# Guard and next threshold in one VectorE operation, and two arrays for the exact heads' transposed tiles, in an attention and mixture-of-experts kernel

## The chip, the cores and the metric

The kernel runs on one core of one Trainium2 chip, in one launch. The metric is device microseconds of one execution; a time is the median of several runs on the same chip. The engines are TensorE (PE in the profile, its weight loads PEld), VectorE (DVE), ScalarE (ACT), GpSimd (POOL) and SyncE (SP, which issues most DMAs). Each engine works through its own instructions in the order in which the program gives them; semaphores make one wait for another.

## The reference

Attention over 2 batches, 8 heads, 576 positions and head dimension 64, then two mixtures of experts. The change lies in the attention alone.

```python
scores = scale * np.matmul(q, k.transpose(0, 1, 3, 2))
thresh = np.max(scores, axis=-1, keepdims=True) - tau
scores = np.where(scores >= thresh, scores, -1000000000.0)
scores = scores - np.max(scores, axis=-1, keepdims=True)
attn = np.exp(scores)
attn = attn / (np.sum(attn, axis=-1, keepdims=True) + 1e-09)
return np.matmul(attn, v).astype(np.float32)
```

The output, 1152 rows of 512, goes through a mixture with 8 experts whose weights come from a softmax with 8 rounds of row and column normalization, and through one with 4 experts whose weights are given. Each expert is relu(x @ w1) @ w2 with 1024 hidden columns. All of it is float32.

## The kernel before, in words

Attention is cut into 72 units of 128 query rows. For each unit the scores against all 576 keys are one tile of two PSUM halves of 288 columns. `units` 0 to 15 are the first 256 query rows of the 8 heads of batch 0 and are called exact: their probabilities and values stay in float32. Units 0 to 3 of these (the first pair of heads, `ws`) have scores that are scaled only afterwards. Units 16 to 35 are the other 320 rows of batch 0, units 36 to 71 the rows of batch 1. These 56 units are not exact: each operand is split into a rounded high part and a remainder (float32r), and products are put together from several matmuls.

`step` (L421) is a software pipeline over the units. In step t unit t is `d` (mask, guard, norm), unit t+1 is `a` (maximum, threshold, exponential), unit t+2 is `nxt` (scores), and units t-2 to t-5 are `x`, `c`, `z`, `y` (transposes and products with the values). The calls in `step` are the order of the work on each engine:

- TensorE: `turn` of `x` (five transposes of the 576 probabilities, four into the PSUM bank et, the last 64 keys into the bank er; there is one bank of each), an exact head's products in three parts (`mix`, L367), filler matmuls, the scores (L282), a non-exact head's products (L374, L376), more filler.
- VectorE: `mask` (L309: scores at or above the threshold keep their exponential, and the sum comes out as an accumulator, which is read by an instruction of its own), `top` (L287, the maximum), `guard` (L313, the sum plus 1e-9), for exact units the threshold (L295, for `ws` units L297 and L298), `norm`'s reciprocal (L317), and then `lo` (L349 and L352, the remainders of the transposed tile), `low` and `rest` of finished heads (L387, L401) and the filler's remainder (L536, tile hl).
- ScalarE: `hi` (L334 copies the transposed tile to SBUF, and after a head's last unit L336 copies the remaining 64 keys), `out` (L384, L398), the exponential (L303 or L305), for the 56 units that are not exact the threshold (L292), the filler's relu (L533, tile hh), and then copies that split operands.
- GpSimd: `norm`'s multiplication (L319), and the remainders of split operands.

`st` holds a unit's maximum, threshold, sum, guarded sum and reciprocal, a column each, in six buffers. All exact heads put their transposed tiles into one array, `e32`: the first head of a pair in its columns 0 to 255, the second in 256 to 511. The heads that are not exact use `eth`, with the remainders in an array that takes `e32`'s place later (for the first such pair, in `tails`).

The filler (`expert_fill`, L527 and L555) is matmul work of the first two experts, which starts at step 20; `pull` gives each step a fixed number of portions, by `few`, `RA1` and `RA2`. What the steps have not done of it is done behind the attention. `cook` splits expert weights on ScalarE (L107) and GpSimd (L109), and `side` issues the loads of weights and calls it.

Of the kernel before, what the change touches and what calls it, by code (L numbers as in the profile page):

```python
# [19 lines left out]
P = 128  # L20
# [9 lines left out]
def attention_two_moe_kernel(ctx, tc, qP, kP, qT, kT, vp, tau, wg, w1, w1s, w2, w2s, dp, m2w1s, m2w2, m2w2s, out):  # L30
# [91 lines left out]
    class Attention:  # L122
# [5 lines left out]
        def __init__(self, pl, ps_s, ps_t, ps_r, ps_m):  # L128
# [7 lines left out]
            self.eth = pl.tile([P, 5, 640], F32R, name="eth")  # L136
            self.e32 = pl.tile([P, 5, 512], F32, tag="etl", name="e32")
            self.etl = None
            self.qz = [pl.tile([P, 3 * D], F32R, name=f"qz{i}") for i in range(2)]
# [145 lines left out]
        def top(self, u):  # L285
            st = u["st"] = self.pl.tile([P, 8], F32, tag="st", name="st", bufs=6)
            V.tensor_reduce(st[:, 0:1], u["sc"][:, :, :HS], axis=AX.XY, op=ALU.max, negate=not u["q"][0][0]["ws"])  # L287

        def line(self, u):
            st = u["st"]  # L290
            if not u["q"][0][0]["exact"]:
                A.activation(st[:, 2:3], st[:, 0:1], AF.Identity, bias=on[:, 1:2], scale=-1.0)  # L292
                return
            if not u["q"][0][0]["ws"]:
                V.tensor_scalar(st[:, 2:3], st[:, 0:1], -1.0, on[:, 0:1], op0=ALU.mult, op1=ALU.subtract)  # L295
                return
            V.tensor_scalar(st[:, 1:2], st[:, 0:1], lin[:, 0:1], None, op0=ALU.mult)  # L297
            V.tensor_scalar(st[:, 2:3], st[:, 0:1], lin[:, 1:2], None, op0=ALU.subtract)  # L298

        def exp(self, u):  # L300
            ex = u["ex"] = self.pl.tile([P, 2, HS], F32, tag="ex", name="ex", bufs=4)
            if u["q"][0][0]["ws"]:
                A.activation(ex, u["sc"][:, :, :HS], AF.Exp, bias=u["st"][:, 1:2], scale=esc)  # L303
            else:
                A.activation(ex, u["sc"][:, :, :HS], AF.Exp, bias=u["st"][:, 0:1])  # L305

        def mask(self, u):
            st, ex = u["st"], u["ex"]
            V.scalar_tensor_tensor(ex, u["sc"][:, :, :HS], st[:, 2:3], ex, op0=ALU.is_ge, op1=ALU.mult,  # L309
                                   accum_out=st[:, 3:4])  # L310

        def guard(self, u):
            V.tensor_scalar(u["st"][:, 4:5], u["st"][:, 3:4], 1e-9, None, op0=ALU.add)  # L313

        def norm(self, u):
            st = u["st"]
            V.reciprocal(st[:, 5:6], st[:, 4:5])  # L317
            exf = u["exf"] = u["ex"].rearrange("p a b -> p (a b)")
            G.tensor_scalar(exf, exf, st[:, 5:6], 1.0, op0=ALU.mult, op1=ALU.mult)  # L319
# [10 lines left out]

        def hi(self, u):
# [1253 lines left out]
```

## Time and profile before

| | |
|---|---|
| median of 3 runs | 1287.21 us (1286.96 to 1287.28) |
| the profiled execution | 1287.24 us, span 1285.5 us |
| TensorE busy | 1268.6 us (99%), 9373 matmuls |
| VectorE busy | 878.0 us (68%), 1843 instructions |
| ScalarE busy | 738.0 us (57%), 1491 instructions |
| GpSimd busy | 897.4 us (70%), 987 instructions |
| granted TensorE clock | 1.00 in all slices |

The attention stage is the first 240 us or so of the span; the mixtures fill the rest. Times in the trace count from the start of the span. A matmul's end in the trace is modelled, so a busy TensorE is not TensorE at its peak. An instruction of VectorE may start while the one before it still shows as busy. A line such as L80 or L85 is a helper's, and the tile names tell what it works on.

### The profile page before, as it was taken

Reading aid. Unit: us, or ns where it says so; the run is one execution under the profiler, and the core shown is the slowest. Engines: PE = TensorE matmul, PEld = TensorE weight load, DVE = VectorE, ACT = ScalarE, POOL = GpSimd, SP = SyncE. Lnnn points to the kernel's source line nnn. Section 1 sums busy time; section 2 is a strip of 40 time slices with the busy share of each in tenths; the row PEclk is TensorE's granted clock in tenths of the full one; section 3 lists DMA queues with packets and bytes.
Section 4 is the critical chain, followed back from the end, with each engine's and each line's share of the span. In section 5 each row is a group of like instructions: output and inputs, shape, how many; then the busy total and the mean of one; then the engine's idle time right before and its main releaser. Section 6 shows DMA issues by size and latency. Waiting matters only on the chain.

```text
span 1285.5 us, 25112 instructions
## 1 busy us (share of the span) xinstructions
PE 1268.6 (99%) x9373; PEld 1209.0 (94%) x9373; DVE 878.0 (68%) x1843; ACT 738.0 (57%) x1491; POOL 897.4 (70%) x987
## 2 busy tenths in 40 slices
PE   8998999999999999999999999999999999999998
PEld 5597988889889999999999999999989999999998
DVE  6798888566637666666666666666745666666667
ACT  7887887423546555554655555466546465556552
POOL 7997987415796767867676786767668578677760
PEclk9999999999999999999999999999999999999999
DMA  5542330101221112211111221111212012111102
GB/s 170 162 126 77 97 98 17 42 1 34 81 67 50 42 42 58 58 34 51 50 42 42 58 59 34 50 50 42 58 38 62 17 53 57 35 55 50 42 18 74
DMA packets 43226, 73.84 MB, mean 57 GB/s; under 512 B 5217, under 2 KB 12513, under 8 KB 43105
## 3 DMA queue, kind: packets, MB, share of 16 engines
q1 hardware_dynamic: 42816, 71.96, 19.6%
q8 instruction: 74, 1.21, 0.4%
q14 instruction: 48, 0.39, 0.1%
q10 hardware_dynamic: 288, 0.28, 0.1%
HBM read 69.86 MB, written 2.36 MB: 56 GB/s over the span
## 4 chain that ended last, share of the span: by engine, by line
PE 89%; DVE 6%; ACT 2%; POOL 1%; issue 1%; DMA 1%; SPq 0%; DVEq 0%; POOLq 0%; ACTq 0%
PE mm L1123 36%; PE mm L1435 33%; PE mm L555 5%; PE mm L527 4%; PE mm L1243 3%; PE mm L282 2%; PE mm L327 2%; DVE ex L309 1%; PE mm L367 1%; DVE st L287 1%; PE mm L376 1%; DVE etl L349 1%; PE mm L374 1%; ACT ex L305 0%; DVE hl L536 0%
## 5 line engine op out<-in xcount | busy, mean ns | idle before, releaser
L85 POOL TENSOR_TENSOR wl<-raw,wh 128x512 fp32r<-128x512 f32 x217 | 282.9, 1310 | 180.2 <-ACT wh L80 166.9
L1223 DVE SCALAR_TENSOR_TENSOR acc<-mm,p,acc 128x256 f32<-128x256 f32 (+1 forms) x428 | 195.3, 508 | 72.5 <-PE mm L1435 59.6
L1435 PE MATMUL mm<-wh,h 128*128 128x256 f32 x960 | 173.6, 280 | 0.0
L1130 ACT COPY snap<-mm 128x576 f32<-128x576 f32 x126 | 80.8, 642 | 157.4 <-DVE mm L1284 77.8
L80 ACT CAST wh<-raw 128x512 fp32r<-128x512 f32 x217 | 133.4, 627 | 47.1 <-PE mm L1435 26.4
L1435 PEld LDWEIGHTS mm<-wh,h 128*128 128x128 f32 x960 | 146.7, 188 | 0.0
L1123 PE MATMUL mm<-xh,wl 128*128 128x288 f32 x672 | 146.3, 299 | 0.3
L1123 PE MATMUL mm<-xh,wh 128*128 128x288 f32 x672 | 143.6, 295 | 0.0
L1123 PE MATMUL mm<-xl,wh 128*128 128x288 f32 x672 | 143.1, 294 | 0.0
L1435 PE MATMUL mm<-wl,h 128*128 128x256 f32 x480 | 134.8, 281 | 0.0
L1435 PE MATMUL mm<-wh,tails 128*128 128x256 f32 x696 | 126.4, 280 | 0.0
L85 POOL TENSOR_TENSOR wl<-sum,wh 128x512 fp32r<-128x512 f32 x82 | 107.0, 1305 | 8.1 <-ACT wh L80 8.1
L1123 PEld LDWEIGHTS mm<-xh,wl 128*128 128x128 f32 x672 | 106.4, 188 | 2.8 <-DVE mm L1143 0.5
L1123 PE MATMUL mm<-xth,wl 128*128 128x288 f32 x504 | 108.3, 296 | 0.1
L1123 PEld LDWEIGHTS mm<-xl,wh 128*128 128x128 f32 x672 | 107.9, 188 | 0.0
L1123 PEld LDWEIGHTS mm<-xh,wh 128*128 128x128 f32 x672 | 107.8, 188 | 0.0
L1123 PE MATMUL mm<-xtl,wh 128*128 128x288 f32 x504 | 107.8, 295 | 0.0
L1123 PE MATMUL mm<-xth,wh 128*128 128x288 f32 x504 | 107.7, 295 | 0.0
L1435 PEld LDWEIGHTS mm<-wh,tails 128*128 128x128 f32 x696 | 106.3, 188 | 0.0
L80 ACT CAST wh<-sum 128x512 fp32r<-128x512 f32 x82 | 51.5, 628 | 85.4 <-POOL sum L820 71.9
L1435 PE MATMUL mm<-wl,tails 128*128 128x256 f32 x348 | 97.4, 280 | 0.0
L1435 PEld LDWEIGHTS mm<-wl,h 128*128 128x128 f32 x480 | 90.3, 188 | 0.4
(242 smaller groups left out, 3489.5 us busy)
## 6 DMA issues: line engine op xcount, KB each, us to landing
raw<-in_w1s SPq DMA_DIRECT2D x56, 256.0 KB, 2.7
raw<-in_w2s SPq DMA_DIRECT2D x48, 256.0 KB, 2.6
raw<-in_w SPq DMA_DIRECT2D x40, 256.0 KB, 3.1
raw<-in_m2w1s SPq DMA_DIRECT2D x32, 256.0 KB, 2.7
raw<-in_m2w2s SPq DMA_DIRECT2D x28, 256.0 KB, 2.6
kr<-in_kT SPq DMA_DIRECT2D x22, 288.0 KB, 3.0
vr<-in_vp SPq DMA_DIRECT2D x24, 160.0 KB, 2.3
qr<-in_qT SPq DMA_DIRECT2D x8, 288.0 KB, 2.9
```

The lines of the kernel that those rows point to most:

```text
L80: A.copy(hi, src)
L85: el.tensor_tensor(lo, src, f(hi), op=ALU.subtract)
L282: T.matmul(sc[:m, hf, :HS], lhsT=q, rhs=kk[:, hf * HS:(hf + 1) * HS], start=i == 0, stop=i == len(ops) - 1)
L287: V.tensor_reduce(st[:, 0:1], u["sc"][:, :, :HS], axis=AX.XY, op=ALU.max, negate=not u["q"][0][0]["ws"])
L327: T.transpose(et[:, kt], exf[:, kt * P:(kt + 1) * P], ident)
L527: T.matmul(ph[:, :n], lhsT=a[:, kt * P:(kt + 1) * P], rhs=x[:, kt, n0:n0 + n], start=i == 0 and kt == 0, stop=i == 2 and kt == KT - 1)
L555: T.matmul(py, lhsT=x, rhs=a, start=i == 0, stop=i == 3 * FT - 1)
L1123: T.matmul(ch[b][:, g, :HS], lhsT=w[:, (2 * g + kt) * P:(2 * g + kt + 1) * P], rhs=operand(u, kt, lo), start=first and j == 0, stop=j == l ...
L1130: A.copy(v[u], m)
L1223: V.scalar_tensor_tensor(a, src, s, a, op0=ALU.mult, op1=ALU.add)
L1243: T.matmul(py, lhsT=hid[x][:, kk, o:o + P], rhs=w[y], start=n == 0, stop=n == 3 * HF - 1)
L1435: T.matmul(m, lhsT=hid(x, kt + ko), rhs=wk[y], start=first and n == 0, stop=n == 5, skip_group_check=True)
```

## The change

The threshold and the guard of all units that are exact but not `ws`, and of all units that are not exact, become one `tensor_tensor` on two columns: it takes the pair (sum of unit t, a constant) minus the pair (-1e-9, negated maximum of unit t+1) and so gives the guarded sum of unit t and the threshold of unit t+1. For this the sums and maxima lie in one tile, `sums`, of six places with eight columns each, in place of `st`; column 2 is set to -1e-9 by a memset and column 1 to the constant at the end of step 0. The threshold of the units that are not exact thereby goes from ScalarE to VectorE. `ws` units keep their separate operations. The tile that `eth` had becomes `e2`, a second array for exact heads: pairs 0 and 2 use `e2`, pairs 1 and 3 `e32`. `eth` is made when the first unit that is not exact is copied, in the place of `e2`. For exact heads the copy of the remaining keys goes from ScalarE (in `hi`) to VectorE (in `lo`).

```diff
--- before.py
+++ after.py
@@ -133,9 +133,11 @@
             self.later, self.late = [], []
             self.iq = self.iv = self.lq = self.lv = 0
             self.xf = {}
-            self.eth = pl.tile([P, 5, 640], F32R, name="eth")
+            self.e2, self.eth = pl.tile([P, 5, 640], F32, tag="eth", name="e2"), None
             self.e32 = pl.tile([P, 5, 512], F32, tag="etl", name="e32")
             self.etl = None
+            self.sums = pl.tile([P, 6, 8], F32, name="sums")
+            G.memset(self.sums[:, :, 2], -1e-9)
             self.qz = [pl.tile([P, 3 * D], F32R, name=f"qz{i}") for i in range(2)]
             for z in self.qz:
                 V.tensor_scalar(z[:, D:2 * D], ident[:, :D], 0.0, None, op0=ALU.mult)
@@ -283,40 +285,41 @@
                              start=i == 0, stop=i == len(ops) - 1)
 
         def top(self, u):
-            st = u["st"] = self.pl.tile([P, 8], F32, tag="st", name="st", bufs=6)
-            V.tensor_reduce(st[:, 0:1], u["sc"][:, :, :HS], axis=AX.XY, op=ALU.max, negate=not u["q"][0][0]["ws"])
-
-        def line(self, u):
-            st = u["st"]
-            if not u["q"][0][0]["exact"]:
-                A.activation(st[:, 2:3], st[:, 0:1], AF.Identity, bias=on[:, 1:2], scale=-1.0)
-                return
-            if not u["q"][0][0]["ws"]:
-                V.tensor_scalar(st[:, 2:3], st[:, 0:1], -1.0, on[:, 0:1], op0=ALU.mult, op1=ALU.subtract)
-                return
-            V.tensor_scalar(st[:, 1:2], st[:, 0:1], lin[:, 0:1], None, op0=ALU.mult)
-            V.tensor_scalar(st[:, 2:3], st[:, 0:1], lin[:, 1:2], None, op0=ALU.subtract)
+            s = self.sums[:, (self.t + 6) % 6]
+            u["max"], u["line"] = s[:, 3:4], s[:, 5:6]
+            V.tensor_reduce(u["max"], u["sc"][:, :, :HS], axis=AX.XY, op=ALU.max, negate=not u["q"][0][0]["ws"])
+
+        def line(self, u, d):
+
+            s = self.sums[:, (self.t + 6) % 6]
+            ws = u and u["q"][0][0]["ws"]
+            if ws or not u:
+                if d:
+                    V.tensor_scalar(s[:, 4:5], s[:, 0:1], 1e-9, None, op0=ALU.add)
+                if ws:
+                    u["bias"] = s[:, 7:8]
+                    V.tensor_scalar(u["bias"], u["max"], lin[:, 0:1], None, op0=ALU.mult)
+                    V.tensor_scalar(u["line"], u["max"], lin[:, 1:2], None, op0=ALU.subtract)
+            else:
+                V.tensor_tensor(s[:, 4:6], s[:, 0:2], s[:, 2:4], op=ALU.subtract)
 
         def exp(self, u):
             ex = u["ex"] = self.pl.tile([P, 2, HS], F32, tag="ex", name="ex", bufs=4)
             if u["q"][0][0]["ws"]:
-                A.activation(ex, u["sc"][:, :, :HS], AF.Exp, bias=u["st"][:, 1:2], scale=esc)
+                A.activation(ex, u["sc"][:, :, :HS], AF.Exp, bias=u["bias"], scale=esc)
             else:
-                A.activation(ex, u["sc"][:, :, :HS], AF.Exp, bias=u["st"][:, 0:1])
+                A.activation(ex, u["sc"][:, :, :HS], AF.Exp, bias=u["max"])
 
         def mask(self, u):
-            st, ex = u["st"], u["ex"]
-            V.scalar_tensor_tensor(ex, u["sc"][:, :, :HS], st[:, 2:3], ex, op0=ALU.is_ge, op1=ALU.mult,
-                                   accum_out=st[:, 3:4])
-
-        def guard(self, u):
-            V.tensor_scalar(u["st"][:, 4:5], u["st"][:, 3:4], 1e-9, None, op0=ALU.add)
+            ex = u["ex"]
+            V.scalar_tensor_tensor(ex, u["sc"][:, :, :HS], u["line"], ex, op0=ALU.is_ge, op1=ALU.mult,
+                                   accum_out=self.sums[:, self.t % 6, 0:1])
 
         def norm(self, u):
-            st = u["st"]
-            V.reciprocal(st[:, 5:6], st[:, 4:5])
+            s = self.sums[:, self.t % 6]
+            V.reciprocal(s[:, 6:7], s[:, 4:5])
             exf = u["exf"] = u["ex"].rearrange("p a b -> p (a b)")
-            G.tensor_scalar(exf, exf, st[:, 5:6], 1.0, op0=ALU.mult, op1=ALU.mult)
+            G.tensor_scalar(exf, exf, s[:, 6:7], 1.0, op0=ALU.mult, op1=ALU.mult)
 
         def turn(self, u):
             eg, exf = u["eg"], u["exf"]
@@ -328,11 +331,18 @@
             c = u["c"] - eg["c0"]
             T.transpose(eg["er"][:D, c:c + P], exf[:, 4 * P:], ident)
 
+        def place(self, hd):
+            if not hd["exact"]:
+                if self.eth is None:
+                    self.eth = self.pl.tile([P, 5, 640], F32R, tag="eth", name="eth")
+                return self.eth
+            return self.e32 if hd["h"] // 2 % 2 else self.e2
+
         def hi(self, u):
             eg, c, et = u["eg"], slice(u["c"], u["c"] + P), u["et"]
-            eth = self.e32 if u["q"][0][0]["exact"] else self.eth
+            eth = self.place(u["q"][0][0])
             A.copy(eth[:, 0:4, c], et)
-            if u["last"]:
+            if u["last"] and not u["q"][0][0]["exact"]:
                 A.copy(eth[:D, 4, eg["c0"]:eg["c0"] + eg["n"]], eg["er"][:D, :eg["n"]])
 
         def low(self, hd):
@@ -345,6 +355,8 @@
         def lo(self, u):
             eg, c, et = u["eg"], slice(u["c"], u["c"] + P), u["et"]
             if u["q"][0][0]["exact"]:
+                if u["last"]:
+                    V.tensor_copy(self.place(u["q"][0][0])[:D, 4, eg["c0"]:eg["c0"] + eg["n"]], eg["er"][:D, :eg["n"]])
                 return
             V.tensor_tensor(self.low(u["q"][0][0])[:, :, c], et, f(self.eth[:, 0:4, c]), op=ALU.subtract)
             if u["last"]:
@@ -364,7 +376,7 @@
                 r0 = (hd["h"] % 2) * D
                 for kt in self.parts(hd)[part]:
                     k = P if kt < 4 else D
-                    T.matmul(pv[r0:r0 + D, :n], lhsT=hd["v"][:k, kt], rhs=self.e32[:k, kt, c], start=kt == 0,
+                    T.matmul(pv[r0:r0 + D, :n], lhsT=hd["v"][:k, kt], rhs=self.place(hd)[:k, kt, c], start=kt == 0,
                              stop=kt == 4)
                 if part == 2:
                     self.lv -= 1
@@ -430,10 +442,7 @@
                 self.mask(d)
             if a:
                 self.top(a)
-            if d:
-                self.guard(d)
-            if a and a["q"][0][0]["exact"]:
-                self.line(a)
+            self.line(a, d)
             if d:
                 self.norm(d)
             for part, u in ((2, y), (1, z), (0, c)):
@@ -453,8 +462,6 @@
                 self.hi(x)
             if a:
                 self.exp(a)
-                if not a["q"][0][0]["exact"]:
-                    self.line(a)
             fill(0, bool(c and c["mix"]))
             if x:
                 self.lo(x)
@@ -612,6 +619,8 @@
         def side():
             if at.t >= -1:
                 fetch(2)
+            if at.t == 0:
+                V.tensor_scalar(at.sums[:, :, 1], at.sums[:, :, 2], 0.0, on[:, 1:2], op0=ALU.mult, op1=ALU.add)
             if at.t >= nA0 - 3 and raws and room[0] and (at.t % 3 < 2 if at.t < nA1 else room[0] > 2 or at.t % 2):
                 room[0] -= 1
                 cook()
```

## Rows read from the trace of the kernel before

**Rows 1.** Part 1 of the page: busy us, share of the span, instructions.

```profile
PE 1268.6 (99%) x9373; PEld 1209.0 (94%) x9373; DVE 878.0 (68%) x1843; ACT 738.0 (57%) x1491; POOL 897.4 (70%) x987
```

**Rows 2.** Windows: length, busy us (instructions) by engine, clock, DMA share, GB/s.

```profile
18.00:60.00 42.00, 41.78 (x223) 25.67 (x221) 31.37 (x99) 37.96 (x78) 39.06 (x45) 1.00 0.51 146
60.00:98.00 38.00, 36.21 (x261) 32.54 (x259) 34.40 (x89) 32.14 (x74) 35.59 (x43) 1.00 0.48 134
98.00:130.00 32.00, 28.73 (x186) 25.18 (x185) 28.27 (x71) 23.96 (x53) 22.32 (x28) 1.00 0.26 73
130.00:178.00 48.00, 48.00 (x325) 45.30 (x324) 42.24 (x109) 38.05 (x83) 43.81 (x74) 1.00 0.34 98
178.00:204.00 26.00, 24.40 (x194) 22.74 (x192) 22.66 (x59) 23.40 (x55) 23.24 (x25) 1.00 0.27 80
204.00:240.00 36.00, 35.84 (x236) 33.00 (x237) 28.21 (x70) 22.41 (x51) 17.77 (x32) 1.00 0.00 1
```

**Rows 3.** Waits of TensorE, 18 to 240 us: total us, times, longest.

```profile
PE mm L327 <- DVE etl L349: 2.9, 7, 0.9
PE mm L282 <- DVE ex L309: 1.9, 3, 1.0
```

**Rows 4.** VectorE in order of time, 4.9 to 6.8 us: start, duration.

```profile
4.93 0.16 DVE L609 TENSOR_TENSOR on<-tau_sb,on 128x1 f32<-128x1 f32 x1
...
6.00 0.76 DVE L287 TENSOR_REDUCE st<-mm 128x1 f32<-128x576 f32 x1 [0.73 <-PE mm L275]
6.79 0.21 DVE L297 TENSOR_SCALAR st<-st,lin 128x1 f32<-128x1 f32 x1
```

**Rows 5.** VectorE in order of time, 184.9 to 191 us.

```profile
184.92 0.75 DVE L287 TENSOR_REDUCE st<-mm 128x1 f32<-128x576 f32 x1
185.59 0.14 DVE L313 TENSOR_SCALAR st<-st 128x1 f32<-128x1 f32 x1
185.77 0.17 DVE L317 RECIPROCAL st<-st 128x1 f32<-128x1 f32 x1
185.85 0.68 DVE L349 TENSOR_TENSOR etl<-mm,eth 128x512 fp32r<-128x512 f32 x1
186.56 0.42 DVE L352 TENSOR_TENSOR eth<-mm,eth 64x256 fp32r<-64x256 f32 x1
...
187.46 0.42 DVE L536 SCALAR_TENSOR_TENSOR hl<-mm,hh 128x256 fp32r<-128x256 f32 x1
187.81 0.81 DVE L309 SCALAR_TENSOR_TENSOR ex<-mm,st,ex 128x576 f32<-128x576 f32 x1
...
188.54 0.75 DVE L287 TENSOR_REDUCE st<-mm 128x1 f32<-128x576 f32 x1
...
190.62 0.42 DVE L536 SCALAR_TENSOR_TENSOR hl<-mm,hh 128x256 fp32r<-128x256 f32 x1 [0.48 <-ACT hh L533]
190.96 0.81 DVE L309 SCALAR_TENSOR_TENSOR ex<-mm,st,ex 128x576 f32<-128x576 f32 x1
```

**Rows 6.** ScalarE in order of time, 189.3 to 190.3 us.

```profile
189.39 0.74 ACT L305 ACTIVATE ex<-mm,st 128x576 f32<-128x576 f32 x1 [0.51 <-DVE st L313]
190.03 0.28 ACT L292 ACTIVATE st<-st,on 128x1 f32<-128x1 f32 x1
190.21 0.37 ACT L533 ACTIVATE hh<-mm 128x256 fp32r<-128x256 f32 x1
```

**Rows 7.** VectorE's groups, 0 to 240 us: busy, mean ns | idle before, releasers.

```profile
L309 DVE SCALAR_TENSOR_TENSOR ex<-mm,st,ex 128x576 f32<-128x576 f32 x72 | 58.6, 815 | 17.1 <-ACT ex L305 6.6 <-ACT st L292 6.2 <-ACT ex L303 3.3
...
L387 DVE TENSOR_TENSOR xl<-mm,xh 64x256 fp32r<-64x256 f32 x8 | 3.3, 418 | 1.3 <-ACT xh L384 1.1
```

**Rows 8.** Waits of all engines, 18 to 60 us.

```profile
DVE ex L309 <- ACT st L292: 2.6, 4, 0.9
```

**Rows 9.** All engines in order of time, 26.6 to 27.4 us.

```profile
26.63 1.08 PE L367 MATMUL mm<-e,vr 128*64 128x256 f32 x4
...
27.33 0.58 ACT L334 COPY e<-mm 128x512 f32<-128x512 f32 x1
```

## The prediction

> **What bounds the kernel now.** I read the busy shares first, then the windows that cut the attention stage into stretches, then who keeps TensorE waiting, then single steps in order of time. The shares show TensorE busy for 1268.6 of 1285.5 us [rows 1]; behind the attention stage (after about 240 us) it has next to no holes, and nothing of the change lies there. Every edit acts in the first 240 us, and a saving counts only where TensorE has a hole to lose. The windows give the holes: 0.22 us in 18 to 60, 1.79 in 60 to 98, 3.27 in 98 to 130, none in 130 to 178, 1.60 in 178 to 204, 0.16 in 204 to 240, in all 7.0 us [rows 2]. That is the most that this change can win there, 0.55% of the run. The waits name what the holes end on: 2.9 us on etl (VectorE's remainder of the transposed tile, which frees the PSUM bank of the next transposes), 1.9 us on the mask (which frees the score bank) [rows 3]. Both are VectorE instructions behind the ones that the change touches. So the question is whether VectorE reaches mask and etl sooner in those stretches.
>
> Two steps show VectorE's round. In the full one it never rests: top 184.92, guard 185.59, reciprocal 185.77, etl 185.85, the remaining keys 186.56, xf, hl 187.46, next mask 187.81 [rows 5]. In the plain one after it hl (190.62) waited for ScalarE's relu: top 188.54, exponential 189.39, threshold 190.03, relu 190.21 [rows 5, 6]. So the full step is bound by VectorE, the plain one by the way over ScalarE, and a change that shifts work from ScalarE to VectorE wins in one kind and loses in the other.
>
> **The change, part by part.**
>
> *The threshold of the 56 non-exact units goes from ScalarE to VectorE.* On ScalarE an instruction of 0.28 us goes; the relu behind it started 0.19 us after it did (190.03 to 190.21), so the relu, and with it hl and the next mask, can come 0.19 us sooner in a plain step [rows 6]. On VectorE guard (0.14) is replaced by a tensor-tensor on two columns. Its own time is near 0.16, which the tensor-tensor on one column took [rows 4]: 0.02 more. But the old guard needed only the mask's sum. It started 0.67 us after top, whose own time is 0.75, so its start was hidden under top's end (184.92 to 185.59) [rows 5]. The new operation needs top's maximum. What such an operation does is shown at the start, where the one that reads top's result came 0.79 us after top (6.00 to 6.79) [rows 4]. So it starts 0.12 us later and lasts 0.02 longer: reciprocal, etl and all behind them come 0.14 us later on VectorE. Bounds: +0.02 if the start still overlaps, +0.14 if not; I take +0.14, since the row at 6.79 is the same pair of operations.
>
> Here a page speaks against my value. The Trainium skill (VectorE: DVE Perf Modes, The DRAIN you can't avoid) says that a VectorE instruction does not start until the pipe of the one before is empty and that a semaphore between two costs nothing extra; a later sentence there lets one that is not held start earlier. By its first sentence the added wait would be free, 0.02 us a step. The trace does not agree with that sentence: guard started 0.08 us before top's record ended, the dependent one 0.03 after [rows 4, 5].
>
> Per kind of step, between mask and mask:
> - plain: the ScalarE way was 0.73 (mask to top) + 0.85 (top to exponential) + 0.64 (to threshold) + 0.19 + 0.41 (relu to hl) + 0.34 (hl to mask) = 3.16 and becomes 2.97. VectorE's own way becomes 0.73 + 0.93 + 0.14 + 0.71 + 0.35 = 2.86 (0.93 is top to etl, 0.71 etl to the next start). So -0.19.
> - full, or with the remaining keys or xf alone: VectorE's own way, +0.14.
> - full steps in which the copies ahead of the exponential make ScalarE late: ScalarE's way gains, VectorE's 0.14 stops it at about -0.13.
> - steps without hl (the filler is in its second layer): 0.73 + 0.85 + 0.64 + 0.28 + 0.1 = 2.6 before; VectorE's way 0.73 + 0.93 + 0.14 + 0.71 = 2.51, so -0.1.
>
> I count the steps by their mask instructions, a pattern of which two stand in [rows 5]. 60 to 98 us: eleven steps; four plain (-0.76), two with a late ScalarE (-0.26), five bound by VectorE, one of them by half (+0.64): -0.4. 98 to 130: the holes at 125 to 127 hang on a chain from TensorE over ScalarE's copy and are unchanged; the four steps from 110 to 121 give -0.19 + 0.14 - 0.1 + 0.14: 0. 130 to 178: TensorE has no hole, 0. 178 to 204: three plain (-0.57), three bound by VectorE (+0.42), two neutral: -0.15. 204 to 240: one late etl, +0.1.
>
> *The exact steps (18 to 60 us).* Guard and threshold, two operations, become one; it starts where the threshold did, so the reciprocal stays within 0.1 us of its place. ScalarE is free of a copy of the remaining keys per head, 8 in all, and its copy into the transposed array no longer waits for the matmuls that read the other pair's. TensorE was busy 41.78 of 42.00 us there [rows 2], so I allow -0.2, what its one hole is worth. VectorE gets 8 copies of 64x256 from PSUM. The trace has no such copy; bounds 0.42 (the subtraction of that shape) and 0.68 (one of twice the columns) [rows 5, 7]; I take 0.42, the same shape. VectorE rested 10.6 of 42 us there [rows 2], after the reciprocal, where the copy goes: nothing on the path. Were that cover gone, it would be 8 x 0.42 = 3.4 us.
>
> *Setup and places.* A memset on GpSimd and one small VectorE operation at step 0, before VectorE's wait for an exponential: 0. The non-exact array now takes the place of one exact array; that one's last reader runs at step 16, the first writer at step 18: no wait. Some tiles move by 192 bytes; no row shows an effect of place, bounds unknown, taken as 0.
>
> Sum: -0.2 - 0.4 + 0 + 0 - 0.15 + 0.1 = -0.65 us. The profiled execution took 1287.24 us (span 1285.5), 0.03 above the median 1287.21. 1287.24 - 0.65 = **1286.6 us**.
>
> **The rivals.**
> - *ScalarE's relief comes through whole.* VectorE's masks waited 6.2 us for the threshold [rows 7], 2.6 of it before 60 us [rows 8], so 3.6 behind. If VectorE has more slack than I count, all of that leaves the holes: 1283.6. For it: the waits are real and TensorE's holes are larger. Against: in full steps VectorE had no gap.
> - *The added wait is free* (the +0.02 bound). Each +0.14 becomes +0.02 and the caps fall: ten steps x 0.12 and some 0.35 from the capped ones, 1.55 better: 1285.0. Against it stand 0.67 and 0.79. This is the result of the page's first sentence.
> - *Slower: VectorE's delay decides everywhere.* The place is top to the two-column operation, the price 0.14 us a step. It decides from the point where VectorE, not the relu, is last at hl also in plain steps; there the margin is 2.97 against 2.86, 0.11 us. Then the 26 steps on such rounds (11 in 60 to 98, 4 and 3 in 98 to 130, 8 in 178 to 204) pay 3.6 us: 1290.9. For it: VectorE is busy 34.4 of 38 us in 60 to 98 [rows 2]. Against: the measured wait at 190.62.
> - *Slower, by a false wait.* All sums, maxima and thresholds now lie in one tile. If waits were kept by tile, the reciprocal would wait for the exponential that reads another column: it would come at 0.85 + 0.74 = 1.6 us after top and not at 1.0, 0.3 to 0.8 us in 26 steps, some 15 us: 1302. Against: the copy into one half of the exact array began at 27.33, while matmuls on its other half ran to 27.71 [rows 9], so waits go by region.
> - *The change doesn't do what it says*, in the exact arrays: TensorE has no hole there, and the time stays in the forecast.
>
> **How the numbers follow.** Forecast 0.56 (its own range 1285.2 to 1287.9), whole relief 0.17, free wait 0.10, VectorE everywhere 0.12, false wait 0.05. What a measurement can tell from no change is about 0.2%, 2.6 us, so within 1284.6 to 1289.8. Faster by more: the whole relief and a part of the free wait and of the forecast's tail, 0.22. Slower: the last two, 0.17, with a little of the tail 0.18. Same: 0.60. The range leaves out part of the whole relief and most of the slow cases: 1283.4 to 1290.4.
>
> **What would show it.** Top to the two-column operation at 0.79 us and to the reciprocal at 0.98 (now 0.67 and 0.85); plain steps near 2.97 us, full ones near 3.76; no threshold on ScalarE; TensorE's holes in 60 to 130 still near 5 us. I am wrong if the two-column operation starts 0.67 after top, if the masks wait for something new, or if holes fall or grow by over 2 us.

## The result: slower by 13.4 us, and the profile after

The changed kernel takes 1300.58 us (median of 4 runs, 1300.15 to 1300.78), the kernel before 1287.15 (4 runs, 1286.96 to 1287.28) on the same chip. The ratio is 1.0104, with a 95% interval of 1.0091 to 1.0116. The forecast of 1286.6 and its range up to 1290.4 are both missed, and by a mechanism that stands among none of the rivals.

The busy shares of the changed kernel, in the columns of [rows 1]:

```profile
PE 1270.9 (98%) x9373; PEld 1207.6 (93%) x9373; DVE 910.9 (70%) x1840; ACT 727.2 (56%) x1427; POOL 897.4 (69%) x988
```

ScalarE lost 64 instructions, the 56 thresholds and the 8 copies, as the change says. VectorE has three instructions less than before and is nevertheless busy for 32.9 us more. No count explains that: some instruction must have become long.

The windows of the changed kernel, in the columns of [rows 2]:

```profile
18.00:60.00 42.00, 41.03 (x217) 24.69 (x216) 39.28 (x95) 34.34 (x65) 38.61 (x43) 1.00 0.50 146
60.00:98.00 38.00, 34.15 (x248) 30.21 (x246) 36.55 (x84) 28.30 (x58) 33.70 (x41) 1.00 0.44 126
...
130.00:178.00 48.00, 43.08 (x292) 39.68 (x293) 45.99 (x98) 34.04 (x66) 40.30 (x70) 1.00 0.30 89
178.00:204.00 26.00, 23.85 (x171) 21.66 (x169) 24.39 (x52) 19.00 (x39) 18.72 (x20) 1.00 0.26 77
204.00:240.00 36.00, 33.66 (x225) 30.21 (x226) 33.21 (x78) 22.80 (x45) 22.78 (x26) 1.00 0.06 16
```

VectorE is now busy for 39.28 of the 42 us from 18 to 60 and for 45.99 of 48 in 130 to 178. TensorE had no hole in 130 to 178 before and has 4.92 us there now. Nearly all the lost time, 12.5 of the 13.4 us, lies in the attention stage: the last mask instruction starts at 242.3 us instead of 229.8, and from there to the end of the span the two kernels take 1056.6 and 1055.7 us.

The longest wait of TensorE on VectorE in 18 to 252 us of the changed kernel (total us, times, longest), which answers to [rows 3]:

```profile
PE mm L330 <- DVE etl L361: 11.0, 17, 1.8
```

The wait on etl, 2.9 us before, is 11.0 now. It is the wait that the prediction named, only longer: etl stands behind the reciprocal, and that behind the new operation. So the groups of VectorE come next (0 to 260 us, columns as in [rows 7]):

```profile
L290 DVE TENSOR_REDUCE sums<-mm 128x1 f32<-128x576 f32 x72 | 54.1, 751 | 0.4 <-PE mm L277 0.4
L304 DVE TENSOR_TENSOR sums<-sums 128x2 f32<-128x2 f32 x68 | 37.7, 555 | 2.3
...
L320 DVE RECIPROCAL sums<-sums 128x1 f32<-128x1 f32 x72 | 11.8, 164 | 2.4
```

The two-column operation, two numbers in each partition, takes 555 ns in the mean, where the prediction had 160. A mean far above the expected time asks for single instances. These are the changed kernel's VectorE and GpSimd in order of time (start, duration), in four stretches:

```profile
80.87 0.87 POOL L85 TENSOR_TENSOR vhl<-vr,vhl 128x320 fp32r<-128x320 f32 x1
81.81 0.19 DVE L85 TENSOR_TENSOR wg<-wg_sb,wg 128x32 fp32r<-128x32 f32 x1
...
125.24 0.74 DVE L290 TENSOR_REDUCE sums<-mm 128x1 f32<-128x576 f32 x1
126.02 0.16 DVE L304 TENSOR_TENSOR sums<-sums 128x2 f32<-128x2 f32 x1
126.22 0.16 DVE L320 RECIPROCAL sums<-sums 128x1 f32<-128x1 f32 x1
...
167.59 0.76 POOL L322 TENSOR_SCALAR ex<-ex,sums 128x576 f32<-128x576 f32 x1
167.74 3.24 DVE L304 TENSOR_TENSOR sums<-sums 128x2 f32<-128x2 f32 x1
168.30 1.44 POOL L85 TENSOR_TENSOR kl<-kr,kh 128x576 fp32r<-128x576 f32 x1
169.67 1.29 POOL L109 TENSOR_TENSOR wl<-raw,wh 128x512 fp32r<-128x512 f32 x1
171.02 0.17 DVE L320 RECIPROCAL sums<-sums 128x1 f32<-128x1 f32 x1
...
186.01 0.75 DVE L290 TENSOR_REDUCE sums<-mm 128x1 f32<-128x576 f32 x1
186.62 1.42 POOL L256 TENSOR_TENSOR qs<-qr,qs 64x576 fp32r<-64x576 f32 x1
186.79 1.26 DVE L304 TENSOR_TENSOR sums<-sums 128x2 f32<-128x2 f32 x1
188.09 0.16 DVE L320 RECIPROCAL sums<-sums 128x1 f32<-128x1 f32 x1
```

Read the ends, start plus duration. At 186.79 the operation starts while GpSimd's L256 runs; GpSimd ends at 188.04, the operation at 188.05. At 167.74 it starts under L322 and ends only after L322, L85 and L109 have all run one behind the other, 3.24 us later (170.96 and 170.98). At 126.02 GpSimd is idle, and it takes 0.16. So the operation is held until GpSimd is through. The time is lost in its own length and not in its start: all 68 start 0.78 or 0.79 us after top, held or not. Over the trace, 43 of the 68 took more than 0.23 us, and each of the 43 started while a GpSimd instruction ran and ended 5 to 21 ns after the end of one. The others took 0.16 to 0.19, at times with GpSimd idle or with less than 0.18 us of its instruction left. The time above 0.16 us each is 37.7 - 68 x 0.160 = 26.8 us. Sorted by the GpSimd instruction that they ended with: 17 with L85 (10.5 us), 14 with L109 (9.7), 6 with L256 (4.9), 4 with L322 (1.0), 2 with L255 (0.7).

The kernel before had shown it, in places that the change doesn't touch: once in the attention stage, and more often behind it. Its VectorE and GpSimd in order of time:

```profile
78.61 0.75 POOL L319 TENSOR_SCALAR ex<-ex,st 128x576 f32<-128x576 f32 x1
78.71 0.69 DVE L85 TENSOR_TENSOR wg<-wg_sb,wg 128x32 fp32r<-128x32 f32 x1
...
252.87 1.39 POOL L820 TENSOR_TENSOR sum<-raw,raw 128x512 f32<-128x512 f32 x1
253.03 1.54 DVE L951 TENSOR_TENSOR sums<-sums 128x288 f32<-128x288 f32 x1
254.61 0.46 DVE L953 TENSOR_TENSOR sums<-sums 128x288 f32<-128x288 f32 x1
```

The instruction at 78.71, a subtraction of 128x32 with both inputs in SBUF, took 0.69 us under a GpSimd instruction there (ends 79.36 and 79.40) and 0.19 in the changed kernel, where GpSimd had ended at 81.74 (81.81 above). Behind the attention 48 operations of 128x288 have both inputs in SBUF: 36 took 0.44 to 0.46 us, and 12 took 0.89 to 1.56, each of them until 0.31 to 0.32 us after the end of a GpSimd instruction, as at 253.03 (ends 254.26 and 254.57). I priced the new operation from the row at 4.93 us [rows 4], the setup, where it happened to run unhindered.

The Trainium skill states the rule (SBUF — State Buffer, Who interferes with whom): a VectorE instruction with two inputs in SBUF contends with a GpSimd instruction that reads SBUF, and the one that comes second is fully blocked until the first is done. The trace agrees, with 0.555 against 0.160 us. That several GpSimd instructions pass one waiting VectorE instruction is more than the Trainium skill's rule by itself gives; it happened once among the 43 (167.74).

### The profile page after: what moved, and what is told of

The parts are those of the page before. It is cut to its first block, busy times and chain, and to the rows that moved or that the text cites. A ratio compares the mean times of both kernels' runs of the same rounds, so it can differ in the third digit from the quotient of the medians.

```text
span 1298.9 us, 25005 instructions
## 1 busy us (share of the span) xinstructions
PE 1270.9 (98%) x9373; PEld 1207.6 (93%) x9373; DVE 910.9 (70%) x1840; ACT 727.2 (56%) x1427; POOL 897.4 (69%) x988
## 4 chain that ended last, share of the span: by engine, by line
PE 83%; DVE 11%; ACT 2%; POOL 2%; issue 1%; DMA 0%; SPq 0%; DVEq 0%; POOLq 0%; ACTq 0%
PE mm L1132 35%; PE mm L1444 33%; PE mm L562 4%; PE mm L534 3%; PE mm L1252 3%; DVE ex L315 2%; DVE sums L290 2%; DVE sums L304 2%; DVE etl L361 1%; PE mm L330 1%; PE mm L284 1%; PE mm L379 1%; DVE hl L543 1%; ACT ex L311 1%; DVE eth L364 0%
## 5 line engine op out<-in xcount | busy, mean ns | idle before, releaser
L85 POOL TENSOR_TENSOR wl<-raw,wh 128x512 fp32r<-128x512 f32 x217 | 282.7, 1309 | 181.0 <-ACT wh L80 167.7
L85 POOL TENSOR_TENSOR wl<-sum,wh 128x512 fp32r<-128x512 f32 x82 | 107.0, 1305 | 8.1 <-ACT wh L80 8.1
```

Source lines behind the costliest of these rows:

```text
L85: el.tensor_tensor(lo, src, f(hi), op=ALU.subtract)
```

## Experiments

The theory, called P in the expectations, is that the operation is held by GpSimd because of how it reads SBUF. The rivals were that two columns or the pair's addresses are slow in themselves, that the arrays or the longer dependency cost the time, and later that two inputs are needed for a hold. In the diffs "-" is the changed kernel's line, unless the text says otherwise. Differences are against the kernel before on the same chip.

### The arrays and VectorE's copies alone

On the kernel before: `place`, `e2` and the copy in `lo` as in the change, `guard`, thresholds and `st` as before.

```
-            eth = self.e32 if u["q"][0][0]["exact"] else self.eth
+            eth = self.place(u["q"][0][0])
```

> The arrays part alone, on the kernel before: two arrays for exact heads, VectorE copies their remaining keys; sums, guard and threshold as before. Theory P (the two-column operation reads both inputs from SBUF and is held until the GpSimd instruction under way has ended): nothing of the 13.4 us is here, 1286.5 to 1287.5 us, the 8 copies at 0.4 us each on VectorE with no new hole on TensorE. Rival A (the arrays, the copies or the tiles moved by 192 bytes carry a share of the loss): 1290 us or more.

Measured: 1287.10 us against 1287.13, ratio 1.0000 (0.9992 to 1.0009). Its first window:

```profile
18.00:60.00 42.00, 41.30 (x221) 24.90 (x218) 34.07 (x107) 35.89 (x71) 39.06 (x45) 1.00 0.49 146
```

VectorE is busy 2.7 us more than in [rows 2], and the time does not move. TensorE is busy 0.48 us less than there, but in the same window it was busy for only 41.11 us in a kernel that keeps the arrays of before (the section on ScalarE's threshold, below), so a hole of this size can't be put down to the arrays. This half of the change shows neither a cost nor a gain.

### The paired operation alone

The changed kernel with `e32` and ScalarE's copy as before, the other half.

```
-            eth = self.place(u["q"][0][0])
+            eth = self.e32 if u["q"][0][0]["exact"] else self.eth
```

> The two-column operation alone, with the arrays as before. Theory P: the whole loss, 1299 to 1302 us, the operation at 0.5 to 0.6 us mean. Rival A: 1290 to 1297 us.

Measured: 1297.99 us, ratio 1.0087 (1.0073 to 1.0101); L304 has a mean of 506 ns, 34.4 us over 68. It fell just below the 1299 that P expected. The pair carries at least 10.9 of the 13.4 us. The other 2.6 us can't be given to the copies: the two intervals overlap, and TensorE's windows differ in 60 to 98 us (36.30 busy here, 34.15 in the changed kernel), where there are no such copies but the held time is 1.7 us here and 4.6 there. Which steps meet a GpSimd instruction shifts with every edit.

### Guard and threshold as two one-column operations

Both stay on VectorE, in the same place; each has one tensor input and a constant.

```
-                V.tensor_tensor(s[:, 4:6], s[:, 0:2], s[:, 2:4], op=ALU.subtract)
+                if d:
+                    V.tensor_scalar(s[:, 4:5], s[:, 0:1], 1e-9, None, op0=ALU.add)
+                V.tensor_scalar(u["line"], u["max"], -1.0, on[:, 0:1], op0=ALU.mult, op1=ALU.subtract)
```

> The changed kernel with the two-column operation taken apart again: guard and threshold as two one-column operations with one SBUF tensor input each, both on VectorE, everything else as changed (one tile for all sums, threshold on VectorE). Theory P: 0.14 and 0.21 us each whatever GpSimd does, reciprocal 0.92 us after top, 1285.5 to 1289 us. Rival D (a VectorE that has to make the threshold behind top, or waits on the shared tile, is what costs): 1297 us or more.

Measured: 1286.46 us (1286.18 to 1288.04), ratio 0.9997 (0.9989 to 1.0006). Its groups (0 to 260 us) and, in order of time, the start of a full step and the plain step behind it. The profile is of the execution of 1288.04 us; its granted clock is 0.96 in 60 to 98 us and 1.00 in the stretch shown:

```profile
L306 DVE TENSOR_SCALAR sums<-sums,on 128x1 f32<-128x1 f32 x68 | 14.6, 214 | 0.0
L305 DVE TENSOR_SCALAR sums<-sums 128x1 f32<-128x1 f32 x68 | 9.7, 143 | 0.0
```

```profile
185.02 0.81 DVE L317 SCALAR_TENSOR_TENSOR ex<-mm,sums,ex 128x576 f32<-128x576 f32 x1
...
188.70 0.81 DVE L317 SCALAR_TENSOR_TENSOR ex<-mm,sums,ex 128x576 f32<-128x576 f32 x1
189.43 0.75 DVE L290 TENSOR_REDUCE sums<-mm 128x1 f32<-128x576 f32 x1
189.55 1.29 POOL L109 TENSOR_TENSOR wl<-raw,wh 128x512 fp32r<-128x512 f32 x1
190.10 0.14 DVE L305 TENSOR_SCALAR sums<-sums 128x1 f32<-128x1 f32 x1
190.22 0.21 DVE L306 TENSOR_SCALAR sums<-sums,on 128x1 f32<-128x1 f32 x1
190.35 0.15 DVE L322 RECIPROCAL sums<-sums 128x1 f32<-128x1 f32 x1
...
191.67 0.81 DVE L317 SCALAR_TENSOR_TENSOR ex<-mm,sums,ex 128x576 f32<-128x576 f32 x1
```

L109 runs from 189.55 to 190.84 over both operations, and neither is held. Of the 68 guards 60 started under a GpSimd instruction, and the longest took 0.147 us; of the thresholds it was 55, and the longest took 0.217. The threshold's constant (`on`) is itself read from SBUF, one number for each partition, and brings no hold. Two VectorE instructions in place of one are 14 us faster here. The step from mask to mask takes 2.97 us (188.70 to 191.67), which is what the prediction worked out for a plain step.

### The same operation with one input in PSUM

The sum (the mask's accumulator) and the constant lie in unused columns of the PSUM bank that holds er. Only the other pair, -1e-9 and the negated maximum, is then read from SBUF.

```
-                V.tensor_tensor(s[:, 4:6], s[:, 0:2], s[:, 2:4], op=ALU.subtract)
+                V.tensor_tensor(s[:, 4:6], self.pairs[:, (self.t + 6) % 6], s[:, 2:4], op=ALU.subtract)
```

> The changed kernel with one of the two inputs of the two-column operation (the pair of sum and constant) in PSUM instead of SBUF; same operation, same columns, same place in the order. Theory P: the operation falls from 0.555 us mean to 0.25 us or less, and the time to 1286 to 1290 us. Rival W (two columns, or their strides, are what is slow) and rival D: it stays at 0.5 us or the time at 1297 us or more.

Measured: 1320.83 us, ratio 1.0261 (1.0247 to 1.0275). The group of the operation (0 to 260 us), and the longest wait of all engines in 18 to 260 us:

```profile
L305 DVE TENSOR_TENSOR sums<-mm,sums 128x2 f32<-128x2 f32 x67 | 10.7, 160 | 2.3
```

```profile
DVE ex L316 <- PE mm L333: 41.8, 46, 2.0
```

The operation is back at 160 ns, as P has it, but the time forecast fails by over 30 us. The mask now writes into the bank into which TensorE's transposes (L333) write, and it waits for them, 41.8 us in all. The experiment took one wait away and put a larger one in. It tells about the operation and nothing about the time.

### The threshold alone as a two-input operation on one column

```
-                V.tensor_tensor(s[:, 4:6], s[:, 0:2], s[:, 2:4], op=ALU.subtract)
+                if d:
+                    V.tensor_scalar(s[:, 4:5], s[:, 0:1], 1e-9, None, op0=ALU.add)
+                V.tensor_tensor(u["line"], s[:, 1:2], u["max"], op=ALU.subtract)
```

> As the changed kernel, but guard is again an operation of its own with one input, and the threshold is a tensor-tensor on ONE column, constant minus negated maximum, both in SBUF. Theory P (two SBUF inputs are held by GpSimd, whatever the width): 0.45 to 0.6 us mean and 1297 to 1303 us. Rival W (two columns are what is slow): 0.16 us and 1286 to 1289 us.

Measured: 1292.88 us, ratio 1.0048 (1.0034 to 1.0062). Its groups, 0 to 260 us:

```profile
L306 DVE TENSOR_TENSOR sums<-sums 128x1 f32<-128x1 f32 x68 | 33.4, 491 | 0.0
L305 DVE TENSOR_SCALAR sums<-sums 128x1 f32<-128x1 f32 x68 | 9.6, 141 | 0.0
```

One column with two inputs in SBUF is held as well (42 of 68, each until 2 to 20 ns after a GpSimd instruction's end), while the guard just ahead of it, with one input, is not. So two columns are not needed for a hold where two inputs come from SBUF. The time came out below P's 1297 to 1303, although the held time, 33.4 - 68 x 0.160 = 22.5 us, is close to that of the paired operation alone (23.5). Of this more below.

### Two columns with one input

The split kernel with the guard over two columns, its second result unused. This asks whether two inputs are needed.

```
-                    V.tensor_scalar(s[:, 4:5], s[:, 0:1], 1e-9, None, op0=ALU.add)
+                    V.tensor_scalar(s[:, 4:6], s[:, 0:2], 1e-9, None, op0=ALU.add)
```

> The taken-apart kernel (guard and threshold each with one SBUF tensor input), but guard now runs over two columns, the second of which is overwritten by the threshold. Theory P in its narrow form (only a second SBUF input is held): 0.15 us, 1286 to 1289 us. Theory P2 (an operation with one SBUF input on an even number of columns is held as well, as the setup operation on six columns at 1.32 us suggests): 0.4 us or more, 1295 us or more.

Measured: 1300.70 us, ratio 1.0108 (1.0094 to 1.0122). Its groups (0 to 260 us) and one instance in order of time:

```profile
L305 DVE TENSOR_SCALAR sums<-sums 128x2 f32<-128x2 f32 x68 | 40.0, 588 | 0.0
L306 DVE TENSOR_SCALAR sums<-sums,on 128x1 f32<-128x1 f32 x68 | 14.6, 214 | 2.4
```

```profile
187.32 1.41 POOL L256 TENSOR_TENSOR qs<-qr,qs 64x576 fp32r<-64x576 f32 x1
187.38 1.38 DVE L305 TENSOR_SCALAR sums<-sums 128x2 f32<-128x2 f32 x1
```

An operation with one input on two columns is held too (43 of 68), until 22 to 35 ns after GpSimd's end; on one column (L306) it isn't. The change's own setup operation, one input on six columns, had shown the same: it ran from 9.85 to 11.17 us, under L85, which ended at 11.14. The narrow form of P, that only two inputs are held, falls. A guard one column wider, whose extra result nobody reads, puts the loss at 13.8 us, where the kernel with the one-column guard has none.

### Without the guard

The reciprocal is taken from the sum itself, ahead of the threshold, which stays a one-column operation on VectorE.

```
-            V.reciprocal(s[:, 6:7], s[:, 4:5])
+            V.reciprocal(s[:, 6:7], s[:, 0:1])
...
-                V.tensor_tensor(s[:, 4:6], s[:, 0:2], s[:, 2:4], op=ALU.subtract)
+                V.tensor_scalar(u["line"], u["max"], -1.0, on[:, 0:1], op0=ALU.mult, op1=ALU.subtract)
```

> Changed kernel in which no operation has two SBUF inputs: the reciprocal takes the mask's sum directly, and the threshold follows it on VectorE as a one-column operation with one tensor input. Left out is the addition of 1e-9 to a sum of at least 1, which does not change a float32. Theory P: reciprocal 0.67 us after top, etl at 0.93 as before, plain steps 2.97 us, full ones 3.6: 1284.5 to 1286.3 us. Rival D (a threshold on VectorE costs): 1288 us or more.

Measured: 1284.98 us (1284.7 to 1286.1), ratio 0.9986 (0.9977 to 0.9995). Two of its windows:

```profile
98.00:130.00 32.00, 29.34 (x191) 26.01 (x190) 29.35 (x75) 22.80 (x43) 23.01 (x28) 1.00 0.26 73
...
178.00:204.00 26.00, 24.98 (x200) 24.00 (x201) 24.79 (x64) 21.93 (x46) 23.38 (x26) 1.00 0.26 80
```

This is faster than both kernels, by 1.9 us against the one before. The gain is not the guard's alone, since the threshold lies on VectorE here as well; the kernel before without its guard was not tried. Each sum holds exp(0) = 1 of the row's maximum, and 1e-9 is below what float32 resolves at 1, so the guard can go. TensorE's holes shrink by 0.6 us in each of the two windows. It is about half of the 3.6 us that the prediction's first rival would have won.

The same with the arrays of the kernel before:

```
-            eth = self.place(u["q"][0][0])
+            eth = self.e32 if u["q"][0][0]["exact"] else self.eth
```

> The kernel without guard and with the one-column threshold on VectorE, but with the arrays of the kernel before (one array for exact heads, ScalarE copies the remaining keys). If the arrays are worth nothing by themselves, as e_arrays showed: 1284.5 to 1285.6 us, the same as e_noguard. If the lighter ScalarE in 18 to 60 us is what gains there: 1286 us or more.

Measured: 1285.28 us, ratio 0.9989 (0.998 to 0.9998). The arrays make no difference here either.

### ScalarE's threshold behind the relu

On the kernel before: the threshold stays on ScalarE and is issued after the filler's relu.

```
             if a:
                 self.exp(a)
-                if not a["q"][0][0]["exact"]:
-                    self.line(a)
             fill(0, bool(c and c["mix"]))
+            if a and not a["q"][0][0]["exact"]:
+                self.line(a)
```

> The kernel before with one edit: ScalarE makes the threshold of the non-exact units behind the filler's relu and not ahead of it. By the step sums of the prediction the relu comes 0.19 us sooner with nothing added on VectorE: plain steps 2.97 us, 1285 to 1286.8 us. If the mask then waits for the threshold instead: 1287 us or more.

Measured: 1287.63 us (1285.99 to 1289.33), ratio 1.0005 (0.9996 to 1.0013): no difference that can be told. Two mask instructions in order of time:

```profile
187.49 0.81 DVE L309 SCALAR_TENSOR_TENSOR ex<-mm,st,ex 128x576 f32<-128x576 f32 x1
...
190.46 0.81 DVE L309 SCALAR_TENSOR_TENSOR ex<-mm,st,ex 128x576 f32<-128x576 f32 x1
```

The plain step takes 2.97 us here, where it took 3.15 before (187.81 to 190.96 in [rows 5]), so the prediction's reading of that step holds: the relu gains its 0.19 us. A part is given back, since the mask waits for the threshold instead: 7.2 us in the profiled execution, 6.2 before [rows 7]. The last mask starts at 229.1 us, 0.7 sooner than before. But the profile is of an execution of 1286.00 us, at the low end of a wide spread, so it does not explain the median; why that shows no gain is open.

### Constants in PSUM, sum and maximum in SBUF

One operation on two columns, as in the change, but the constant pair lies in PSUM, is written once, and serves all steps. The sum and the negated maximum lie side by side in SBUF and are subtracted from it; the guarded sum comes out negative, and GpSimd's multiplication by -1.0 sets it right.

```
-                V.tensor_tensor(s[:, 4:6], s[:, 0:2], s[:, 2:4], op=ALU.subtract)
+                V.tensor_tensor(s[:, 4:6], self.pair, s[:, 2:4], op=ALU.subtract)
...
-            G.tensor_scalar(exf, exf, s[:, 6:7], 1.0, op0=ALU.mult, op1=ALU.mult)
+            G.tensor_scalar(exf, exf, s[:, 6:7], -1.0, op0=ALU.mult, op1=ALU.mult)
```

> The changed kernel with the two-column operation turned round: two constants that lie in PSUM, written once, minus the pair (sum, negated maximum) in SBUF; the guarded sum comes out negated and GpSimd's multiplication takes that back. One operation of two columns as in the change, with one SBUF input and, unlike the earlier PSUM kernel, nothing written to PSUM in a step. Theory P: 0.16 to 0.2 us each, and what the prediction's step sums say without the hold, 1286 to 1289 us; waits on the PSUM bank, which transposes also write, can add some. Rival D (the threshold behind top on VectorE costs): 1295 us or more.

Measured: 1288.26 us (1287.79 to 1289.96), ratio 1.0014 (1.0004 to 1.0023). The group (0 to 260 us) and one instance in order of time:

```profile
L304 DVE TENSOR_TENSOR sums<-mm,sums 128x2 f32<-128x2 f32 x68 | 10.9, 160 | 11.0 <-PE mm L332 4.4
```

```profile
189.92 1.29 POOL L109 TENSOR_TENSOR wl<-raw,wh 128x512 fp32r<-128x512 f32 x1
190.81 0.16 DVE L304 TENSOR_TENSOR sums<-mm,sums 128x2 f32<-128x2 f32 x1
```

This is the experiment that isolates the cause: same engine, operation, shape and place, the same sum and maximum to wait for, and one of its two inputs out of SBUF. 59 of the 68 started under a GpSimd instruction, and none took over 0.162 us. 12.0 of the 13.4 us are gone. The remaining 1.4 us go with a new idle time of 11.0 us before the operation, 4.4 of it, in five waits, for the transposes that write into the same bank; in most other steps it starts 0.86 us after top, where it did so after 0.78 in the changed kernel. That the 1.4 us come from this idle time was not tried.

### GpSimd's subtractions as memsets

The changed kernel with GpSimd's 32 subtractions L109 replaced by memsets of the same shape.

```
-            G.tensor_tensor(lo, raw, f(hi), op=ALU.subtract)
+            G.memset(f(lo), 0.0)
```

> The changed kernel, VectorE untouched; on GpSimd the 32 subtractions that make the remainders of the first experts' weights (two SBUF inputs, 1.28 us each, 14 of the 45 holds and 9.7 of the 26.8 us) become memsets, so these remainders are left out of the products. Theory P, the hold lasts for a GpSimd instruction that reads SBUF: the operation falls to about 0.4 us mean, the time to 1292 to 1298 us. Rival D (VectorE's own order is the cost): no change of VectorE's operation, 1299 us or more.

Measured: 1292.72 us, ratio 1.0047 (1.0033 to 1.006), as expected. (The 45 holds of the expectation count two of 0.185 and 0.194 us, which the 43 above leave out.) Its groups of both engines (0 to 260 us), and an instance in order of time:

```profile
L304 DVE TENSOR_TENSOR sums<-sums 128x2 f32<-128x2 f32 x68 | 28.2, 415 | 2.3
...
L109 POOL MEMSET wl<- 128x512 f32 x32 | 16.8, 525 | 0.0
```

```profile
162.26 0.52 POOL L109 MEMSET wl<- 128x512 f32 x1
162.59 0.16 DVE L304 TENSOR_TENSOR sums<-sums 128x2 f32<-128x2 f32 x1
```

The operation at 162.59 starts under a memset that runs to 162.78, and takes 0.16: a GpSimd instruction that only writes does not hold it. Four of the 68 started under such a memset, and each took 0.161 us. No held operation ends with a memset; 32 are still held, for 17.3 us, by GpSimd's other instructions. With fewer held, the loss is 5.9 us and not 13.4. A part of this difference may come from GpSimd itself, which is relieved of 32 x (1.284 - 0.525) = 24 us, and in the kernel before 29 of the 32 lie in windows in which it was busy for 89 to 94% of the time [rows 2]. So this experiment shows what the operation does, and its time alone would not show the cause.

### Held time against lost time

Held time is the group's busy time less 68 x 0.160; the loss is against the kernel before on the same chip:

| kernel | mean, ns | held, us | loss, us |
|---|---|---|---|
| two one-column operations | 143 and 214 | 0 | -0.7 |
| constants in PSUM | 160 | 0 | 1.4 |
| memsets on GpSimd | 415 | 17.3 | 5.9 |
| threshold alone, two inputs | 491 | 22.5 | 6.0 |
| pair alone | 506 | 23.5 | 10.9 |
| the change | 555 | 26.8 | 13.4 |
| two columns, one input | 588 | 29.1 | 13.8 |

The two kernels in which nothing is held are at -0.7 and 1.4 us, the five with a hold lose 5.9 to 13.8, and more held time goes with more loss (5.9 and 6.0 can't be told apart, nor 13.4 and 13.8; with memsets GpSimd also does less work). It is not a proportion. That slack swallows a part, such as the 0.48 us ahead of hl at 190.62 [rows 5], is likely but not shown. Why the threshold alone loses 6.0 us and the pair alone 10.9 at nearly the same held time is open; it was not tried.

## Why the prediction was wrong

*The step that failed* is a term of the sum, in the words of the prediction: "Its own time is near 0.16, which the tensor-tensor on one column took". It measured 0.555 in the mean, because the operation of the row at 4.93 us ran with GpSimd idle and 43 of the 68 new ones did not. The error is 0.39 us a step, 26.8 us, of which 13.4 reached the end. The cost was bounded on its start (0.02 to 0.14) and not on its length, although the page of before had GpSimd at 70% and the trace had two-input operations beside it that were held: the one of 128x32 at 78.71, and 12 of the 48 of 128x288 behind the attention.

*What held.* The operation starts 0.78 us after top, and where it isn't held the reciprocal comes after 0.98 (125.24, 126.02, 126.22), as forecast, so the added wait is not free. The plain step became 2.97 us in the kernel with two one-column operations, where nothing is held; the full step there took 3.68 (185.02 to 188.70) instead of 3.76, as its reciprocal comes 0.92 us after top. That kernel came out 0.67 us under the one before, where the sum gave 0.65. This is no confirmation of the sum: the interval (0.9989 to 1.0006) holds no change as well, and in the kernel nearest to the priced one, a fused operation that nothing holds (constants in PSUM), the time is 1.4 us longer than before. What the runs bear out are the starts, the length of the plain step, and that without a hold the change is small.

*The arrays* show neither a gain nor a loss, 1287.10 against 1287.13; the 0.2 us that the sum gave them is too small to be told in an interval of 0.9992 to 1.0009. *Setup* was put at 0: its VectorE operation took 1.32 us, held by GpSimd like the others, and what it cost was not tried. The copy of 64x256 from PSUM took 0.40 us, against 0.42 taken, and VectorE's rest covered it where the arrays ran alone.

*The rivals.* "VectorE's delay decides everywhere" has the right direction, and it named the point from which VectorE decides (0.11 us of margin in plain steps). But its price, 0.14 us a step, is that of the later start; the loss came from the operation's length, 0.39 us a step in the mean, which took the time well past its 1290.9. "The false wait" gave 1302, near the result by accident: the reciprocal comes 0.98 us after top where GpSimd is idle, not 1.6, and the split kernel keeps the one tile and loses nothing. "The whole relief" and "the added wait is free" are out by the rows above. The prediction's own sign for being wrong, holes that grow by over 2 us, is what the windows show: from 0 to 4.92 us in 130 to 178 alone.

## What to carry to other kernels

Price a new instruction by its two engines: for a VectorE operation that reads two tensors from SBUF, or one from SBUF to SBUF over two or more columns, look up whether GpSimd is at work beside it, and take its length from a row where GpSimd runs, up to the length of GpSimd's instructions and at times of several. On the path that sets the end here, two one-column operations with constants beat one fused operation (1286.46 against 1300.58 us), and an input in PSUM freed the fused one. The kernels with such an input, which wait for that bank's other writers, were 1.4 us slower than the one before with constants there, and 33.7 with an accumulator. Better still, ask whether the operation is needed: the two kernels without the guard are the only ones whose gain, 1.9 and 1.6 us, is clear of the spread.

## What the runs showed of the hardware that was not expected

- A small size is no protection: two numbers in each partition waited up to 3.24 us. Several GpSimd instructions can run, one behind the other, while it waits (three at 167.74; up to four in the other kernels).
- A held operation with two inputs ends the later after GpSimd the wider it is: 2 to 20 ns at one column, 5 to 21 at two, 41 at 32 (one instance), 0.31 to 0.32 us at 288. So what is held seems to be its way through the columns; this is inferred from these sizes and was not tried.
- One input is enough where the operation goes from SBUF to SBUF over two columns (0.588 us in the mean), and on one column it is not held (0.143 and 0.214).
- GpSimd's memset, 0.525 us long, held none of the four operations that started under it. The Trainium skill (SBUF — State Buffer, Who interferes with whom) limits the contention of two-input operations to GpSimd instructions that read SBUF, and these rows agree.
- GpSimd is not slowed by the operation that waits for it: L85 on 128x576 took 1.44 us at 168.30, and 1.42 in the mean of 22. It can itself be held where VectorE was first: in the kernel before, L85 on 128x512 took 1.28 to 1.33 us in 328 instances and 1.50 to 1.72 in nine, and these nine are the ones that began while a VectorE operation of 128x288 with both inputs in SBUF ran.
- An accumulator that is written into a PSUM bank in which TensorE's transposes write waits for them, 41.8 us in all over 46 times; the profile infers this from semaphores, so it is the order that the program keeps; whether the memory needs it was not tried.
